# Batch 0 of a fused attention and two-layer kernel: causal mask moved into a TensorE matmul

## The chip, the cores and the metric

One core of a Trainium2 chip runs the whole program in one launch. The metric is device time in microseconds (us). The engines are called by the names of the profile: PE (TensorE matmuls), PEld (its weight loads), DVE (VectorE), ACT (ScalarE), POOL (GpSimd), SP (the queue that issues the DMAs).

## The reference

Attention over 4 batches, 8 heads, 576 positions and 64 columns a head, with a bias made of a running sum, then two feed-forward layers on the result (512 to 1536 gated to 512, then 512 to 2048 to 512). The part that the change touches:

```python
s_pos = np.maximum(s, 0.0)
cum = np.cumsum(s_pos, axis=-1)
bias = -(cum[:, :, :, None] - cum[:, :, None, :])
scores = np.where(causal, -1000000000.0, scores + np.minimum(bias, 0.0))
scores = scores - np.max(scores, axis=-1, keepdims=True)
attn = np.exp(scores)
attn = attn / (np.sum(attn, axis=-1, keepdims=True) + 1e-09)
return np.matmul(attn, v)
```

`causal` is true where the key comes after the query.

## The kernel before

The program has three stages on one timeline. First comes the attention of batch 0 alone (the opening). Then the first layer of batch b runs on PE with the attention of batch b + 1 woven in. The second layer closes. The change is in the opening and in one helper.

**Units and slots.** Two heads make a pair, a pair is cut into half A (query tiles 0, 1 and 2 of `TILES`: 64, 128 and 128 queries, keys 0 to 320) and half B (tiles 3 and 4, 128 queries each, keys 0 to 576). Batch 0 has 8 such units, A and B by turns. `body` (lines 837 to 858) walks through slots 0 to 9 with an order written out by hand for every engine (`manual_schedule`); each engine takes its instructions in that order. Slot u (`first_slot`, line 763) does three things at once: scores of unit u, transposes of unit u - 1, values of unit u - 2. An even slot therefore has A scores, B transposes and A values, an odd slot B scores, A transposes and B values.

**The way of one unit.** `masks` (line 192) lets POOL copy the running sum `c` into a tile `e` with everything after the query replaced by a huge negative number (`affine_select`, one instruction a tile and head; in batch 0 over the full width of the tile). `score_mm` (line 206) multiplies queries by keys on PE; the two heads have 64 rows each and run side by side in the two halves of the array, in fp32, so each matmul is two passes in the trace. `score_min` (line 223) adds scores and `e` on DVE and finds the row's extreme value, `expo` (line 243) takes the exponential and the row sum on ACT, `inverse` (line 259) adds up and inverts the sum on DVE, `normal` (line 283) scales the rows on POOL. `turn_mm` (line 289) transposes the result on PE (L302 over the full array, L309 into 64-column halves of it), `turned` (line 319) copies it out of PSUM on ACT and DVE, `value_mm` (line 329) multiplies by the values, and `x_high` and `x_low` split the result into two parts (ACT, then DVE).

**Weights.** Beside this, the first weight block (chunk 0) is unpacked from 64-bit numbers in four pieces (`decode`, `unpack`, line 406: first step on ACT at L409, second on ACT at L410, two on DVE at L412 and L415) after slots 2, 3, 5 and 6, and cut into a high and a low part (`w_cut`, line 491) after slots 4 and 7. `gate` (line 540; its matmuls stand in `mm3`, L522 to L524) begins the first layer when slot 9 starts.

Slot 7 (`u == H - 1`) has an order of its own at its end: the copies of slot 6's transposes (`turned`), then the DVE part of a decode, then `inverse` of tile 4, then `normal` of tile 4 on POOL.

Of the kernel before, what the change touches and what calls it, by code (L numbers as in the profile page):

```python
# [8 lines left out]
F32 = mybir.dt.float32  # L9
F32R = mybir.dt.float32r  # L10
U32 = mybir.dt.uint32
AF = mybir.ActivationFunctionType
ALU = mybir.AluOpType
# [53 lines left out]
def kernel(  # L67
# [42 lines left out]
    def copy(eng, out, in_, scale=1.0):  # L110
        if eng == "a":
            act_last[:] = [nc.scalar.activation(out=out, in_=in_, func=AF.Copy, scale=scale).ins]  # L112
        elif eng == "v":
            nc.vector.tensor_scalar(out=out, in0=in_, scalar1=scale, scalar2=None, op0=ALU.mult)
        else:
            nc.gpsimd.tensor_scalar(out=out, in0=in_, scalar1=scale, scalar2=1.0, op0=ALU.mult, op1=ALU.mult)
# [30 lines left out]


    st = {}
    first_v, first_z, sums = [], [], []  # L150

    def zeros():
        for n in range(2):
            t = zero_p.tile([P, P], F32, tag=f"v0_{n}", name="vz")
            nc.vector.memset(t, 0.0)
            first_v.append(t)
        first_z.append(zero_p.tile([P, P], F32, tag="z0", name="z0"))
        nc.vector.memset(first_z[0], 0.0)
        for n in range(6):
            sums.append(zero_p.tile([P, 2, 2], F32, tag=f"l{n}", name="ls"))  # L160
            nc.vector.memset(sums[n], 1.0e-9)
# [30 lines left out]
    def masks(b, g, half, tiles=None):  # L192
        c = st[b, g, "qkc"][1]
        es = st.setdefault((b, g, half, "e"), {})
        for i in HALF[half][0] if tiles is None else tiles:
            q0, r = TILES[i]
            g0, wd = (GATE[i] if b > 0 else 0), q0 + r
            e = e_p.tile([P, 2, S], F32, tag="e", name="e")
            for hd in range(2):
                nc.gpsimd.affine_select(  # L200
                    out=e[:r, hd, g0:wd], in_=c[:r, hd, g0:wd], pattern=[[-1, wd - g0]], compare_op=ALU.is_ge,
                    fill=-8.0 * QMASK, base=q0 - g0, channel_multiplier=1,
                )
            es[i] = e

    def score_mm(b, g, half):
        t = st[b, g, "qkc"][0]
        if b == 0:
            banks = [[ps_m.tile([P, 512], F32, tag="m", name="psc") for _ in range(2)] for _ in range(2)]
        else:  # L210
            banks = [ps_a.tile([P, 2, 512], F32, tag="a", name="psc") for _ in range(2)]
            banks = [[p[:, 0], p[:, 1]] for p in banks]
        st[b, g, half, "s"] = banks
        for i, bank, o, c0, n in PACK[half]:
            q0 = TILES[i][0]
            for hd in range(2):
                d0 = hd * D
                nc.tensor.matmul(  # L218
                    out=banks[bank][hd][:, o : o + n], lhsT=t[d0 : d0 + D, 0, q0 : q0 + P],
                    rhs=t[d0 : d0 + D, 1, c0 : c0 + n], start=True, stop=True,  # L220
                )

    def score_min(b, g, half, i):
        c, e, banks = st[b, g, "qkc"][1], st[b, g, half, "e"][i], st[b, g, half, "s"]
        r, g0 = TILES[i][1], (GATE[i] if b > 0 else 0)
        m = [None, None]
        for k, bank, o, c0, n in PACK[half]:
            if k != i:
                continue
            for hd in range(2):  # L230
                for k0, end, gate in ((c0, min(g0, c0 + n), c), (max(g0, c0), c0 + n, e)):
                    if k0 >= end:
                        continue
                    m2 = sm_p.tile([P, 1], F32, tag="m", name="m")
                    nc.vector.tensor_tensor_reduce(  # L235
                        out=e[:r, hd, k0:end], in0=banks[bank][hd][:r, o + k0 - c0 : o + end - c0],
                        in1=gate[:r, hd, k0:end], scale=-0.125,
                        scalar=3.0e38 if m[hd] is None else m[hd][:r], op0=ALU.add, op1=ALU.min, accum_out=m2[:r],
                    )
                    m[hd] = m2  # L240
        st[b, g, half, "m", i] = m
# [38 lines left out]
            else:  # L280
                copy("g", z[:r, hd * D : hd * D + D], e[:r, hd, :D], f)

    def normal(b, g, half, i):
        r, e, rl = TILES[i][1], st[b, g, half, "e"][i], st[b, g, half, "l", i]
        for hd in range(2 if i > 0 or b == 0 else 0):
            x = e[:r, hd, D if b > 0 else 0 : sum(TILES[i])]
            copy("g", x, x, rl[:r, hd : hd + 1])

    def turn_mm(b, g, half):
        tiles, base, n = HALF[half]  # L290
# [28 lines left out]
    def turned(b, g, half, k):  # L319
        n = HALF[half][2]  # L320
        ps, _, pt = st[b, g, half, "p"]
        pt[k] = pt_p.tile([P, 2, 512], F32, tag="pt", name="pt")
        w = WIDE[half][k]
        if w is None:
            copy("av"[k], pt[k][:, 0, :n], ps[k][:, 0, :n])
        else:
            copy("av"[k], pt[k][:, :, :w], ps[k][:, :, :w])
# [35 lines left out]
    def x_low(b, g, half):  # L363
        _, base, n = HALF[half]
        xp, acc = xin[b][g][:, :, base : base + n], st.pop((b, g, half, "x"))
        nc.vector.tensor_tensor(out=xp[:, 1], in0=acc[:, :n], in1=xp[:, 0].bitcast(F32), op=ALU.subtract)
# [38 lines left out]

    def unpack(zz, t, k, part="av"):
        lo, hi = t[:, :, 0], t[:, :, 1]
        if "a" in part:
            nc.scalar.activation(out=zz, in_=hi.bitcast(F32), func=AF.Copy, scale=2.0**-112)  # L409
            nc.scalar.activation(out=k, in_=lo, func=AF.Copy, scale=0.937 * 2.0**-29)  # L410
        if "v" in part:
            nc.vector.scalar_tensor_tensor(  # L412
                out=k, in0=zz.bitcast(U32), scalar=3, in1=k, op0=ALU.logical_shift_left, op1=ALU.bitwise_or
            )
            nc.vector.scalar_tensor_tensor(  # L415
                out=zz.bitcast(U32), in0=hi, scalar=0x80000000, in1=k, op0=ALU.bitwise_and, op1=ALU.bitwise_or
            )
# [345 lines left out]
    def first_slot(u):  # L763
        x = units[u] if u < H else None
        y = units[u - 1] if 1 <= u <= H else None
        z = units[u - 2] if 2 <= u <= H + 1 else None
        tiles = HALF[x[2]][0] if x else []
        after = HALF[units[u + 1][2]][0]
        if x:
            if u > 0:  # L770
                fetch(u)
            score_mm(*x)
            if u < H - 1:
                masks(*units[u + 1], after[:1])
        if z:
            value_mm(*z)
        if y:
            turn_mm(*y)
        for k, i in enumerate(tiles):
            score_min(*x, i)  # L780
            expo(*x, i)
            if z and k == (1 if x[2] == "A" else 0):
                x_high(*z)
            if z and k == len(tiles) - 1:
                x_low(*z)
            if k > 0:
                inverse(*x, tiles[k - 1])
                if u < H - 1:
                    first_keys(*x, tiles[k - 1])
                normal(*x, tiles[k - 1])  # L790
        if z and not x:
            x_high(*z)
            x_low(*z)
        if u == H - 1:
            turned(*y, 0)
            turned(*y, 1)
        if u - 1 in DECODE:
            decode(0, DECODE.index(u - 1), "v")
        if u == H - 1:
            inverse(*x, tiles[-1])  # L800
        if y and u != H - 1:
            turned(*y, 0)
            turned(*y, 1)
        if x:
            if u < H - 1:
                inverse(*x, tiles[-1])
                masks(*units[u + 1], after[1:])
                first_keys(*x, tiles[-1])
            normal(*x, tiles[-1])

    def w_ahead(c):
        wst.pop(c - 1, None)
# [7 lines left out]
    def body():  # L820
# [16 lines left out]
        for u in range(H + 2):  # L837
            if u == H + 1:
                for e in range(2):
                    decode(1, e)  # L840
                gate(0, 0, 0, *both[0])
            first_slot(u)
            if u in DECODE:
                decode(0, DECODE.index(u), "a")
            if u == H:
                masks(*units[H])
            if u in SPLIT:
                w_cut(0, SPLIT.index(u))
            if u == H - 1:
                for i in HALF["B"][0]:  # L850
                    first_keys(*units[u], i)
            if u == SPLIT[0]:
                w_piece(1, 0)
            if u == SPLIT[1]:
                for i in range(1, 4):
                    w_piece(1, i)
            if u >= H:
                w_store(0, u - H)
# [209 lines left out]
```

## Time and profile before

| | us |
|---|---|
| median of the three runs shown (1008.34, 1010.0, 1375.38) | 1010.0 |
| the profiled execution's own time | 1007.44 |
| its span, first to last instruction | 1005.7 |
| PE busy | 990.5 (98%) |
| DVE, ACT, POOL busy | 561.8, 521.8, 594.2 |

The profile is of one execution. A row of the timeline gives the start and the length of a run of like instructions on one engine; for PE the end is modelled and matmuls overlap, so work is read from the start of one row to the start of the next. A granted clock of 1.00 is 2.4 GHz, 0.50 is 1.2 GHz.

### The profile page before, as it was taken

To read this page: it belongs to the slowest core of one execution; us is meant where nothing else is said; L and a number is where in the kernel's file an instruction comes from. 1 tells how busy PE (TensorE), PEld (TensorE's weight loads), DVE (VectorE), ACT (ScalarE), POOL (GpSimd) and SP (SyncE) were. 2 spreads that over 40 slices of the span, in tenths; PEclk is the share of its full clock that TensorE was granted. 3 is DMA by queue.
4 is the path that set the end of the run, shared out by engine and by line. 5 is a ranking of instruction groups with operands and counts; after the bars stand their busy time and mean duration, and the time that the engine had idled before them with its cause. 6 is when DMAs were issued, how large, how long until landed. Compare 5 with 4: busy or idle time off the path is not lost.

```text
span 1005.7 us, 19494 instructions
## 1 busy us (share of the span) xinstructions
PE 990.5 (98%) x6924; PEld 930.9 (93%) x6924; DVE 561.8 (56%) x1408; ACT 521.8 (52%) x1266; POOL 594.2 (59%) x749
## 2 busy tenths in 40 slices
PE   8989999999999999999999999999999999999998
PEld 6578899899898899899899999999999999999998
DVE  5877667635635545545542223366666667665555
ACT  5869878525755535665542543244534335543333
POOL 6966757605866646756551665356567458674445
PEclk9999999999999999999999999999999999999999
DMA  8789789757798799776768676797767866896662
GB/s 234 203 251 340 250 302 282 256 181 266 262 302 269 257 320 309 277 245 230 260 235 315 253 293 247 276 386 290 293 230 281 318 223 247 297 342 233 244 223 106
DMA packets 81618, 267.17 MB, mean 266 GB/s; under 512 B 9904, under 2 KB 29360, under 8 KB 66160
## 3 DMA queue, kind: packets, MB, share of 16 engines
q1 hardware_dynamic: 81376, 265.73, 75.7%
q8 instruction: 54, 0.88, 0.3%
q14 instruction: 44, 0.36, 0.1%
q10 hardware_dynamic: 144, 0.20, 0.1%
HBM read 208.15 MB, written 57.75 MB: 264 GB/s over the span
## 4 chain that ended last, share of the span: by engine, by line
PE 89%; ACT 3%; DVE 2%; issue 2%; DMA 2%; POOL 2%; POOLq 0%; SPq 0%; DVEq 0%; ACTq 0%
PE pgv L522 9%; PE pgv L523 8%; PE pgv L524 8%; PE pu L668 6%; PE pu L664 6%; PE pu L667 6%; PE po L709 6%; PE po L710 6%; PE po L711 6%; PE po L522 5%; PE po L523 5%; PE po L524 5%; PE pv L351 4%; PE psc L218 4%; PE ptr L302 3%
## 5 line engine op out<-in xcount | busy, mean ns | idle before, releaser
L522 PE MATMUL pgv<-xt,wt 128*128 128x288 f32 x768 | 230.1, 300 | 1.6 <-DVE u L533 1.3
L523 PE MATMUL pgv<-xt,wt 128*128 128x288 f32 x768 | 226.6, 295 | 0.0
L524 PE MATMUL pgv<-xt,wt 128*128 128x288 f32 x768 | 226.5, 295 | 0.0
L641 POOL TENSOR_TENSOR h<-u,h 128x384 fp32r<-128x384 f32 x72 | 74.8, 1039 | 142.0 <-ACT h L112 134.1
L522 PEld LDWEIGHTS pgv<-xt,wt 128*128 128x128 f32 x768 | 144.5, 188 | 13.2 <-DVE m L235 6.3
L523 PEld LDWEIGHTS pgv<-xt,wt 128*128 128x128 f32 x768 | 144.6, 188 | 0.0
L524 PEld LDWEIGHTS pgv<-xt,wt 128*128 128x128 f32 x768 | 144.5, 188 | 0.0
L112 ACT ACTIVATE h<-u 128x288 fp32r<-128x288 f32 (+1 forms) x168 | 79.7, 474 | 94.8 <-DVE u L534 93.7
L536 POOL TENSOR_TENSOR h<-u,h 128x288 fp32r<-128x288 f32 x96 | 79.8, 834 | 82.3 <-ACT h L112 78.5
L522 PE MATMUL po<-h,wt 128*128 128x288 f32 x384 | 114.8, 299 | 0.0
L523 PE MATMUL po<-h,wt 128*128 128x288 f32 x384 | 113.1, 294 | 0.0
L524 PE MATMUL po<-h,wt 128*128 128x288 f32 x384 | 113.0, 294 | 0.0
L709 PE MATMUL po<-h,wt 128*128 128x384 f32 x336 | 112.4, 335 | 0.0
L710 PE MATMUL po<-h,wt 128*128 128x384 f32 x336 | 112.3, 334 | 0.0
L711 PE MATMUL po<-h,wt 128*128 128x384 f32 x336 | 112.3, 334 | 0.0
L668 PE MATMUL pu<-x,wt 128*128 128x384 f32 x330 | 111.7, 339 | 0.0
L664 PE MATMUL pu<-x,wt 128*128 128x384 f32 x330 | 111.7, 339 | 0.0
L667 PE MATMUL pu<-x,wt 128*128 128x384 f32 x330 | 111.7, 339 | 0.0
L641 POOL TENSOR_TENSOR h<-t,h 128x384 fp32r<-128x384 f32 x96 | 107.0, 1134 | 5.5 <-ACT h L112 5.5
L255 ACT ACTIVATE e<-e,m 64x64 f32<-64x64 f32 (+4 forms) x160 | 88.3, 554 | 30.6 <-DVE m L235 29.8
L670 ACT ACTIVATE s<-pu 128x384 f32<-128x384 f32 x48 | 23.6, 492 | 149.6 <-PE pu L668 149.6
L720 DVE TENSOR_TENSOR acc<-po,acc 128x384 f32<-128x384 f32 x144 | 76.8, 557 | 36.2 <-PE po L711 35.6
(114 smaller groups left out, 2192.0 us busy)
## 6 DMA issues: line engine op xcount, KB each, us to landing
wt<-w_d SPq DMA_DIRECT2D x54, 1024.0 KB, 7.0
wt<-wu_d SPq DMA_DIRECT2D x48, 1024.0 KB, 9.1
wt<-wu_d SPq DMA_DIRECT2D x47, 768.0 KB, 6.5
r<-in_w_dram SPq DMA_DIRECT2D x36, 512.0 KB, 6.4
w_d<-wt SPq DMA_DIRECT2D x18, 1024.0 KB, 8.3
r<-in_w_dram SPq DMA_DIRECT2D x64, 256.0 KB, 7.2
qkr<-in_qk_dram SPq DMA_DIRECT2D x32, 288.0 KB, 8.3
cumb<-cum_d SPq DMA_DIRECT2D x15, 576.0 KB, 9.4
```

Source lines behind the costliest of these rows:

```text
L255: nc.scalar.activation(out=e[:r, hd, :wd], in_=e[:r, hd, :wd], func=AF.Exp, bias=m[hd][:r], scale=-1.0, accum_out=put[hd],)
L522: nc.tensor.matmul(out=ps[:, :n], lhsT=a, rhs=xh, start=(k == 0), stop=False)
L523: nc.tensor.matmul(out=ps[:, :n], lhsT=a, rhs=xl, start=False, stop=False)
L524: nc.tensor.matmul(out=ps[:, :n], lhsT=c, rhs=xh, start=False, stop=(k == last))
L536: engines[LO[ph]].tensor_tensor(out=lo, in0=u, in1=hi.bitcast(F32), op=ALU.subtract)
L641: nc.gpsimd.tensor_tensor(out=h[:, 1], in0=u, in1=h[:, 0].bitcast(F32), op=ALU.subtract)
L664: nc.tensor.matmul(out=o, lhsT=a, rhs=x[:, 0, kk], start=fresh and kk == 0, stop=False, skip_group_check=True)
L667: nc.tensor.matmul(out=o, lhsT=a, rhs=x[:, 1, kk], stop=False, **more)
L668: nc.tensor.matmul(out=o, lhsT=c, rhs=x[:, 0, kk], stop=kk == 1, **more)
L709: nc.tensor.matmul(out=ps, lhsT=a, rhs=h[:, 0], start=fresh, stop=False, skip_group_check=True)
L710: nc.tensor.matmul(out=ps, lhsT=a, rhs=h[:, 1], stop=False, **more)
L711: nc.tensor.matmul(out=ps, lhsT=c, rhs=h[:, 0], stop=e == 1, **more)
```

## The change

In batch 0 POOL no longer makes masked copies of the running sum. Two constant tiles are made at the start: an identity and a triangle (0 up to the query, -8 x 2^30 after it), both rounded to fp32r. After the scores of each block that holds the diagonal, PE adds identity x triangle to the 64 or 128 columns on the diagonal, for each head, over the full 128 rows of the array. DVE then reads the running sum `c` itself. The first step of the four chunk 0 decodes goes from ACT to POOL. At the end of the opening, the inverse of the last tile of slot 7 stands ahead of the transposes' copies, its second head is scaled on ACT, and the second `w_cut` of chunk 0 goes from behind slot 7 into slot 8.

```diff
+        tri = z_p.tile([P, P], F32, tag="z", name="tri")
+        nc.gpsimd.affine_select(
+            out=tri, in_=first_z[0], pattern=[[-1, P]], compare_op=ALU.is_ge, fill=-8.0 * 2.0**30, base=0,
+            channel_multiplier=1,
+        )
+        for src in (ident, tri):
+            diag.append(z_p.tile([P, P], F32R, tag="z", name="diag"))
+            nc.vector.tensor_scalar(out=diag[-1], in0=src, scalar1=1.0, scalar2=None, op0=ALU.mult)
...
-            g0, wd = (GATE[i] if b > 0 else 0), q0 + r
+            g0, wd = GATE[i], q0 + r
             e = e_p.tile([P, 2, S], F32, tag="e", name="e")
-            for hd in range(2):
+            for hd in range(2 if b > 0 else 0):
                 nc.gpsimd.affine_select(
...
+            lo, end = max(q0, c0), min(q0 + TILES[i][1], c0 + n)
+            for hd in range(2 if b == 0 and lo < end else 0):
+                nc.tensor.matmul(
+                    out=banks[bank][hd][:, o + lo - c0 : o + end - c0], lhsT=diag[0], rhs=diag[1][:, lo - q0 : end - q0],
+                    start=False, stop=True, skip_group_check=True,
+                )
...
-        r, g0 = TILES[i][1], (GATE[i] if b > 0 else 0)
+        r, g0 = TILES[i][1], GATE[i] if b > 0 else S
...
-    def normal(b, g, half, i):
+    def normal(b, g, half, i, eng="gg"):
...
-            copy("g", x, x, rl[:r, hd : hd + 1])
+            copy(eng[hd], x, x, rl[:r, hd : hd + 1])
...
+        if part == "a":
+            copy("g", zz, hi.bitcast(F32), 2.0**-112)
+        elif "a" in part:
+            nc.scalar.activation(out=zz, in_=hi.bitcast(F32), func=AF.Copy, scale=2.0**-112)
         if "a" in part:
-            nc.scalar.activation(out=zz, in_=hi.bitcast(F32), func=AF.Copy, scale=2.0**-112)
             nc.scalar.activation(out=k, in_=lo, func=AF.Copy, scale=0.937 * 2.0**-29)
...
+        if u == H:
+            w_cut(0, 1)
         if u == H - 1:
+            inverse(*x, tiles[-1])
             turned(*y, 0)
             turned(*y, 1)
         if u - 1 in DECODE:
             decode(0, DECODE.index(u - 1), "v")
-        if u == H - 1:
-            inverse(*x, tiles[-1])
...
-            normal(*x, tiles[-1])
+            normal(*x, tiles[-1], "gg" if u < H - 1 else "ga")
...
-            if u in SPLIT:
-                w_cut(0, SPLIT.index(u))
+            if u == SPLIT[0]:
+                w_cut(0, 0)
```

On PE, from the scores of slot 0 to the first transposes (`psc` are scores in PSUM, `qkr` queries and keys, `ptr` transposes), before the change:

```order
L218 MATMUL psc<-qkr 128x64 x2
L218 MATMUL psc<-qkr 128x192 x2
L218 MATMUL psc<-qkr 128x320 x2
L218 MATMUL psc<-qkr 128x448 x2
L218 MATMUL psc<-qkr 128x64 x2
L218 MATMUL psc<-qkr 128x512 x2
L302 MATMUL ptr<-ident,e 128x128 x6
```

and after it (`diag` are the two constant tiles):

```order
L226 MATMUL psc<-qkr 128x64 x2
L232 MATMUL psc<-diag 128x64 x2
L226 MATMUL psc<-qkr 128x192 x2
L232 MATMUL psc<-diag 128x128 x2
L226 MATMUL psc<-qkr 128x320 x2
L232 MATMUL psc<-diag 128x128 x2
L226 MATMUL psc<-qkr 128x448 x2
L232 MATMUL psc<-diag 128x128 x2
L226 MATMUL psc<-qkr 128x64 x2
L232 MATMUL psc<-diag 128x64 x2
L226 MATMUL psc<-qkr 128x512 x2
L232 MATMUL psc<-diag 128x64 x2
```

Each pair of score matmuls is followed by a pair of mask matmuls: six in two slots, so 24 pairs or 48 matmuls in the opening.

On POOL, in slots 3 to 5 (`e<-e,rl` scales rows, `e<-cumb` makes a mask, `wt<-wraw,wt` is the low part of `w_cut`), before the change:

```order
L116 TENSOR_SCALAR e<-e,rl 128x576 x2
L200 AFFINE_SELECT e<-cumb 128x448 x2
L116 TENSOR_SCALAR e<-e,rl 64x64 x2
L116 TENSOR_SCALAR e<-e,rl 128x192 x2
L200 AFFINE_SELECT e<-cumb 128x576 x2
L116 TENSOR_SCALAR e<-e,rl 128x320 x2
L501 TENSOR_TENSOR wt<-wraw,wt 128x1024
L200 AFFINE_SELECT e<-cumb 64x64 x2
L116 TENSOR_SCALAR e<-e,rl 128x448 x2
L200 AFFINE_SELECT e<-cumb 128x192 x2
L200 AFFINE_SELECT e<-cumb 128x320 x2
L116 TENSOR_SCALAR e<-e,rl 128x576 x2
```

and after it (`wraw<-r` is the decode's first step):

```order
L116 TENSOR_SCALAR e<-e,rl 128x576 x2
L116 TENSOR_SCALAR wraw<-r_201 128x512
L116 TENSOR_SCALAR e<-e,rl 64x64 x2
L116 TENSOR_SCALAR e<-e,rl 128x192 x2
L116 TENSOR_SCALAR e<-e,rl 128x320 x2
L518 TENSOR_TENSOR wt<-wraw,wt 128x1024
L116 TENSOR_SCALAR e<-e,rl 128x448 x2
L116 TENSOR_SCALAR e<-e,rl 128x576 x2
```

The mask instructions are gone from between the scalings.

On DVE, at the end of slot 7 (`l` and `rl` are row sums and their inverses, `pt` a transposes' copy, `dk` and `wraw` a decode), before the change:

```order
L366 TENSOR_TENSOR xt<-pv,xt 128x256
L265 TENSOR_REDUCE l<-ls 128x2
L268 RECIPROCAL rl<-l 128x2
L114 TENSOR_SCALAR pt<-ptr 128x320
L412 SCALAR_TENSOR_TENSOR dk<-wraw,dk 128x512
L415 SCALAR_TENSOR_TENSOR wraw<-r_197,dk 128x512
L265 TENSOR_REDUCE l<-ls 128x2
L268 RECIPROCAL rl<-l 128x2
```

and after it:

```order
L380 TENSOR_TENSOR xt<-pv,xt 128x256
L279 TENSOR_REDUCE l<-ls 128x2
L282 RECIPROCAL rl<-l 128x2
L279 TENSOR_REDUCE l<-ls 128x2
L282 RECIPROCAL rl<-l 128x2
L114 TENSOR_SCALAR pt<-ptr 128x320
L429 SCALAR_TENSOR_TENSOR dk<-wraw,dk 128x512
L432 SCALAR_TENSOR_TENSOR wraw<-r_205,dk 128x512
```

The second sum and inverse, those of the last tile, now stand ahead of the copy and the decode.

## Rows read from the trace of the kernel before

**Rows 1.** Stretches: length, then busy time (instructions) of PE, PEld, DVE, ACT, POOL; clock, DMA

```profile
100.00:1005.70 905.70, 900.91 (x6248) 862.22 (x6246) 486.86 (x1150) 448.27 (x1079) 523.59 (x620) 1.00 0.75 267
```

**Rows 2.** Waits between 8.5 and 62 us: us in total, times, longest

```profile
PE ptr L302 <- POOL e L116: 5.1, 8, 1.4
POOL e L116 <- DVE rl L268: 4.6, 3, 2.4
```

**Rows 3.** Timeline of PE in the opening: start, length, instruction, count, wait before

```profile
8.54 1.36 PE L218 MATMUL psc<-qkr 64*128 64x64 f32 x12
...
14.85 0.33 PE L302 MATMUL ptr<-ident,e 128*128 128x128 f32 x1 [1.43 <-POOL e L116]
...
17.10 2.51 PE L218 MATMUL psc<-qkr 64*128 64x64 f32 x12
...
20.89 2.01 PE L302 MATMUL ptr<-ident,e 128*128 128x128 f32 x14
...
23.41 2.10 PE L218 MATMUL psc<-qkr 64*128 64x448 f32 x12
...
35.78 2.10 PE L218 MATMUL psc<-qkr 64*128 64x448 f32 x12
37.81 1.73 PE L351 MATMUL pv<-pt,vrb 128*64 128x256 f32 x16
...
39.91 0.88 PE L302 MATMUL ptr<-ident,e 128*128 128x128 f32 x6
...
41.80 1.36 PE L218 MATMUL psc<-qkr 64*128 64x64 f32 x12
43.09 0.76 PE L351 MATMUL pv<-pt,vz 128*64 128x320 f32 x4
...
44.43 0.44 PE L302 MATMUL ptr<-ident,e 128*128 128x128 f32 x2
...
48.11 2.10 PE L218 MATMUL psc<-qkr 64*128 64x448 f32 x12
...
55.48 0.76 PE L351 MATMUL pv<-pt,vz 128*64 128x320 f32 x4 [0.60 <-DVE pt L114]
...
61.82 0.61 PE L522 MATMUL pgv<-xt,wt 128*128 128x288 f32 x1
```

**Rows 4.** Stretches of the opening and behind it, columns as in rows 1

```profile
16.20:19.60 3.40, 3.40 (x22) 2.20 (x23) 1.27 (x8) 1.94 (x6) 3.25 (x9) 0.50 1.05 338
...
60.60:63.90 3.30, 3.30 (x18) 2.81 (x17) 1.88 (x2) 2.83 (x5) 3.30 (x12) 0.50 1.02 427
```

**Rows 5.** POOL by form between 8 and 61 us: busy us, mean ns

```profile
L200 POOL TENSOR_SCALAR_AFFINE_SELECT e<-cumb 128x576 f32<-128x576 f32 x8 | 5.1, 662 | 0.2 <-PE ptr L309 0.2
L200 POOL TENSOR_SCALAR_AFFINE_SELECT e<-cumb 128x448 f32<-128x448 f32 x8 | 4.7, 610 | 0.0
```

**Rows 6.** PE around the scores of batch 1 between two fp32r runs

```profile
74.58 0.29 PE L524 MATMUL pgv<-xt,wt 128*128 128x288 f32 x1
74.80 1.36 PE L218 MATMUL psc<-qkr 64*128 64x64 f32 x12
76.08 0.40 PE L522 MATMUL pgv<-xt,wt 128*128 128x288 f32 x1
76.32 0.29 PE L523 MATMUL pgv<-xt,wt 128*128 128x288 f32 x1
76.45 0.29 PE L524 MATMUL pgv<-xt,wt 128*128 128x288 f32 x1
```

**Rows 7.** The forms of decode and scaling up to 130 us

```profile
L409 ACT ACTIVATE wraw<-r 128x512 f32<-128x512 f32 x22 | 14.3, 668 | 2.4 <-POOL wt L501 1.3 <-DMA r<-in_w_dram 0.8 <-issue 0.3
...
L116 POOL TENSOR_SCALAR e<-e,rl 128x512 f32<-128x512 f32 x4 | 2.7, 707 | 0.0
```

**Rows 8.** POOL at the end of the opening

```profile
57.29 1.99 POOL L116 TENSOR_SCALAR e<-e,rl 128x576 f32<-128x576 f32 x2 [1.70 <-DVE rl L268]
```

**Rows 9.** Waits of PE between 62 us and the end

```profile
PE pgv L522 <- DVE u L533: 1.3, 1, 1.3
```

More of the change, by code (lines that the diff above doesn't have):

```diff
@@ L149 @@
     st = {}
-    first_v, first_z, sums = [], [], []
+    first_v, first_z, sums, diag = [], [], [], []
     def zeros():
```

## Prediction

> **What bounds the kernel now.** I read the stretches first. From 100 us to the end PE is busy for 900.91 of 905.70 us at clock 1.00 [rows 1], so nothing that the change does to POOL, ACT or DVE there can show; only the opening, up to the first matmul of the first layer at 61.82 us, has anything to give. The waits of that opening come next: PE waits for POOL's scaling 5.1 us in all, and POOL in its turn 4.6 us for DVE's inverse [rows 2]. Then the timeline of PE, read from start to start [rows 3]. A pair of slots lasts 12.37 us (23.41 to 35.78). Taken where PE hardly waits, an even slot is A scores 1.29 (41.80 to 43.09), A values 1.34 (to 44.43) and B transposes 2.52 (20.89 to 23.41), together 5.15; an odd slot is B scores 2.03 (35.78 to 37.81), B values 2.10 (to 39.91) and A transposes 1.89 (to 41.80), together 6.02. So 11.17 of the 12.37 us are PE's own work, and only 1.2 us a pair is a wait that POOL could give back. That is the point to see: POOL ends the waits, but PE stands right behind it. The rest of what is lost lies at the two ends: 1.43 us before the transposes at 14.85 [rows 3], and twice a stretch at clock 0.50, that is 1.2 GHz, from 16.2 to 19.6 and from 60.6 to 63.9 us, each after PE had stood waiting for transposes' inputs [rows 4].
>
> **The masks taken from POOL.** In batch 0 each tile has two selects, 40 in all, in five widths of eight each. The two widest forms alone cost 5.1 and 4.7 us [rows 5], 2.4 us a pair of slots. PE gets its 1.2 us a pair from this and no more. In the first slots it counts for more: the last scaling of slot 0 stood behind two selects of 0.66 us [rows 5], so the transposes that wait at 14.85 [rows 3] and their followers can go up to 1.3 us sooner; I take 0.7, since the scores in front of them end later.
>
> **The masks put on PE.** 48 matmuls are added in 24 pairs, three pairs a slot. No fp32r matmul of 128 columns is in the trace, and none that cuts into the scores, so I build its price from the places where PE goes from full-height fp32r matmuls to the two half-height rows of scores and back [rows 6]. A stream of 288 columns takes 0.13 us from start to start (76.32 to 76.45). Before the scores it takes 0.22 (74.58 to 74.80): 0.09 us to empty the array. After the scores the first takes 0.24 (76.08 to 76.32): 0.11 more, because its weights are not loaded ahead. So a mask pair costs 0.09 to enter, 0.11 for its first weights, 0.11 for the second weights (a second load of that length behind the first), and 0.06 for 128 columns at the rate of 0.13 for 288: 0.37 us. The way back to scores costs 0.09 and about 0.10 for the scores' weights. The third pair of a slot has no way back, since the values that follow change the form of the array anyway. A slot: 3 x 0.37 + 2 x 0.19 = 1.49, less 0.03 for each pair of 64 columns and about 0.1 where the scores' weights were waited for already: 1.36. Eight slots: 10.9 us more on PE. It is on the path, as an odd or even slot of PE then lasts 7.38 and 6.51, a pair 13.9 us, above the 12.37 of now. Other engines have more room than before, so no wait is added on top.
>
> The bounds of this price. Below: both mask matmuls cost a weight load each and nothing for the change of form, 0.22 a pair and 5.3 us in all. Above: a narrow fp32r matmul runs at the rate of fp32, whose 128-column passes take 0.11 each and need two; a pair is then 0.6 us with its entry, 0.2 to 0.27 more, and the whole 5.6 us more, 16.5 us. I take 10.9, since the fp32r rows [rows 6] are the nearest of kind and their price of change is measured.
>
> On the change of form itself the Trainium skill (TensorEngine Tiling (Array Packing), Key Properties) says that switching the tiling mode drains TensorE. By the drain alone, without exposed weights, 24 pairs would cost some 5 us less and this would be the faster rival below; the trace has both parts, 0.09 and 0.11 us.
>
> The constants cost nothing: one select on POOL and two small copies on DVE at the start, which nothing waits for until the first scores at 8.54 [rows 3].
>
> **Decode on POOL.** ACT loses four instructions of 668 ns [rows 7], some 0.6 us each in a row of others. POOL gets four of the same size: 128x512 takes 707 ns there [rows 7], perhaps twice that with every second word read. Against 9.8 us taken off in two forms alone, 3 to 6 us on POOL is hidden behind PE's own work. If PE were not the bound, ACT's 2.4 us could count as a gain, or POOL's 6 as a loss of what exceeds the masks taken away. No DMA changes its place in the opening's queue; the loads of the raw pieces now wait for POOL as well, which is done before DVE's part.
>
> **The last slots.** Now slot 7's inverse stands behind a copy and a decode, so POOL scales the last tile from 57.29 to 59.28, after 1.70 us of waiting [rows 8]. That is 9.1 us after the last scores (48.11 + 2.03) [rows 3]. Without the 1.70 of waiting and with one head on ACT (1.0 less) it is 6.4 us at most. The new scores end at 54.2 (below), so the rows are there by 60.6 at the latest, and PE comes to them at 60.1, with the other tile's transposes first: at most a few tenths late, taken as nothing. The 0.60 us for the copy before the values at 55.48 [rows 3] stays. The second `w_cut` is queued in slot 8 on ACT ahead of the copy of the last transposes. It lies beside 2.52 us of transposes on PE, and its result is wanted by the 13th matmul of the first layer, 12 x 0.13 = 1.6 us later, so I cost it at nothing; if that cover is gone, the cost is what it is late.
>
> **The sum.** Starts of the slots' scores, before and then after: slot 0 8.54 and 8.54; slot 1 11.2 after; slot 2 17.10 and 16.5 (A transposes from 14.6, at full clock); slot 3 23.41 and 23.0; then 7.38 and 6.51 in turn to slot 7 at 50.8 (48.11 before). There 3.39 for scores (2.03 + 1.36), 2.10, 1.89, the wait of 0.60, 1.34 and 2.52: the first layer begins at 62.6 against 61.82, 0.8 us later. PE has then worked without a long wait, so I expect clock 1.00 where it was 0.50 from 60.6 to 63.9 [rows 4]: half of 3.3 us back, 1.65. Net -0.9 us. Against the profiled 1007.44 that is 1006.5. The two ordinary runs shown are 0.9 and 2.6 above the profiled one (1008.34, 1010.0, the latter the median); I add the smaller, 0.9: **1007.4 us**, no change that a measurement would tell (2% of this kernel, some 20 us, is about what one can).
>
> **The rivals.**
> 1. Slower: the mask matmuls run at fp32's rate (0.27 us more for a pair of 128 columns). For it: their columns are fewer than those of any fp32r matmul in the trace. Against: the same type streams 288 columns in 0.13. It makes the first layer start at 68.2, net +4.7, with the 0.9 some 1013. It decides from 0.04 us more a mask pair than I took.
> 2. Faster: the change of form is nearly free, because the weights of the mask are the same in all 48 and its drain hides. For it: POOL's waits do go. Against: rows 6. Net -6.5, some 1001.8.
> 3. The time regained is lost behind the opening: at about 97 us PE waits 1.3 us for DVE [rows 9], and the weights of the first layer come by a DMA queue that is full from 60.6 to 63.9 (1.02) [rows 4]. Or PE still stands long enough that the clock falls as before. Either leaves 0 to +0.8, 1008.3 to 1009.1.
>
> **Chances.** Forecast 0.45, rival 1 0.2, rival 2 0.2, rival 3 0.15. All four lie within 2%: nothing here reaches 20 us either way, since the opening's PE work before masks is some 43 of its 53.3 us (four of each kind above, three B values). Only something unseen leaves the band: 0.015 faster, 0.97 within, 0.015 slower. The range takes rivals 1 and 2 in: 1000.5 to 1013.5; the forecast's own is 1004 to 1010.
>
> **What would show it.** Right: a pair of slots near 13.9 us with no wait of PE for POOL, 0.09 and 0.11 us around each mask pair, the first layer at 62 to 63, clock 1.00 after it. Wrong: a pair of slots under 12.4 us (rival 2), or mask matmuls 0.2 us apart (rival 1), or the 0.50 clock still there (rival 3).

## The result and the profile after

The changed kernel is slower by 0.9%, clear of the noise but inside 2%: 1017.47 us median of 12 runs (1012.24 to 1025.7) against 1009.01 for the kernel before, a ratio of 1.0089 [1.007, 1.0107]. The forecast was 1007.4 with a range from 1000.5 to 1013.5. The profiled execution took 1017.69 us, its span 1015.9 us against 1005.7. The traces lie further apart (10.2 us) than the medians (8.5), because the profiled execution of the kernel before, 1007.44 us, is faster than all 12 of its other runs.

First the part that came out as forecast. PE's timeline over one pair of slots, where the clock was full (start and length; read from start to start):

```profile
27.73 1.02 PE L226 MATMUL psc<-qkr 64*128 64x448 f32 x4
28.68 0.44 PE L232 MATMUL psc<-diag 128*128 128x128 f32 x2
29.05 0.44 PE L226 MATMUL psc<-qkr 64*128 64x64 f32 x4
...
33.26 0.88 PE L316 MATMUL ptr<-ident,e 128*128 128x128 f32 x6
34.30 0.92 PE L323 MATMUL ptr<-ident,e 64*64 64x64 f32 x12 [0.16 <-DVE l L279]
...
41.73 1.02 PE L226 MATMUL psc<-qkr 64*128 64x448 f32 x4
```

From one odd slot's scores to the next it is 14.00 us (27.73 to 41.73; forecast 13.9, [rows 3] give 12.37). A mask pair of 128 columns takes 0.37 (28.68 to 29.05), as was built from [rows 6]. And the 5.1 us that PE waited for POOL [rows 2] are gone: no such wait of PE is among those of the opening (8.5 to 65 us). There the others now wait, DVE for PE and POOL behind DVE:

```profile
engine line waited for: us in total, times, longest us
POOL e L116 <- DVE rl L282: 14.1, 9, 4.7
...
DVE e L249 <- PE psc L232: 10.2, 9, 4.4
```

Then the part that did not. The stretches of PE in the changed kernel, cut at slot 0, the first transposes, slots 3, 5 and 7, the first matmul of the first layer and the 217th (columns: stretch, length, busy, granted clock, DMA share, GB/s):

```profile
core 0: us, PE busy (x), PEclk, DMA share, GB/s
8.91:18.81 9.90, 9.90 (x37) 0.56 0.92 293
18.81:27.73 8.92, 8.88 (x71) 0.91 1.06 225
27.73:41.73 14.00, 13.80 (x115) 1.00 0.56 160
41.73:55.72 13.99, 13.79 (x114) 1.00 0.45 141
55.72:68.02 12.30, 11.14 (x96) 1.00 0.71 214
68.02:113.10 45.08, 39.57 (x287) 0.96 0.84 289
```

There are two losses. The scores and masks of slots 0 and 1 ran at 0.56 of full speed with PE busy all the time (9.90 of 9.90 us). And from the first layer's start to its 217th matmul it took 45.08 us with 5.5 us of idle time. In the kernel before the same matmuls took 11.29 + 28.89 = 40.18 us; its stretches (PE's busy time stands first, the clock third from the end):

```profile
61.82:73.11 11.29, 11.29 (x86) 10.52 (x85) 10.51 (x14) 7.64 (x14) 6.49 (x11) 0.91 0.72 243
73.11:102.00 28.89, 27.36 (x203) 24.37 (x202) 22.35 (x78) 25.38 (x71) 19.90 (x28) 1.00 0.93 325
```

So the first layer began 6.2 us late (68.02 against 61.82) and lost 4.9 us more by the 217th matmul. Those 11.1 us hold the whole loss; behind that matmul the two kernels run nearly alike, the changed one 0.9 us shorter, and the spans end 10.2 us apart.

### The profile page after: what moved, and what is told of

It is laid out like the page before. It is cut to its first block, busy times and chain, and to the rows that moved or that the text cites. A ratio compares the mean times of both kernels' runs of the same rounds, so it can differ in the third digit from the quotient of the medians.

```text
span 1015.9 us, 19484 instructions
## 1 busy us (share of the span) xinstructions
PE 1003.3 (99%) x6972; PEld 939.3 (92%) x6972; DVE 560.9 (55%) x1410; ACT 521.6 (51%) x1263; POOL 583.2 (57%) x713
## 4 chain that ended last, share of the span: by engine, by line
PE 92%; DMA 2%; ACT 2%; POOL 1%; DVE 1%; issue 1%; SPq 0%; DVEq 0%; POOLq 0%; ACTq 0%
PE pgv L539 9%; PE pgv L541 9%; PE pgv L540 9%; PE pu L681 6%; PE pu L685 6%; PE pu L684 6%; PE po L726 6%; PE po L728 6%; PE po L727 6%; PE po L539 5%; PE pv L365 5%; PE psc L226 5%; PE po L540 5%; PE po L541 5%; PE ptr L316 3%; DMA r<-in_w_dram 1%
## 5 line engine op out<-in xcount | busy, mean ns | idle before, releaser
L116 POOL TENSOR_SCALAR e<-e,rl 128x128 f32<-128x128 f32 (+8 forms) x135 | 72.9, 553 | 65.0 <-DVE rl L282 47.5
```

## The experiments

The theory at this point had two parts: full-height mask pairs cost what was forecast but let the clock fall at the start, and something in the reordered end costs PE time behind the opening. The rivals: the decode on POOL is to blame, or weights and not the change of form are the price.

**One part at a time.** `masks_only` keeps the masks on PE and takes back the other two parts; `rest_only` is its opposite. The core of `masks_only`:

```diff
-        if part == "a":
-            copy("g", zz, hi.bitcast(F32), 2.0**-112)
...
-        if u == H:
-            w_cut(0, 1)
```

and of `rest_only`:

```diff
-            for hd in range(2 if b > 0 else 0):
+            for hd in range(2):
                 nc.gpsimd.affine_select(
```

> Only the masks go to PE; the decode's first step is on ACT again and the last slots have their old order. Theory (the masks' price on PE, and a lower clock at the start): a pair of slots lasts 14.0 us as in the full change, the clock falls to 0.50 soon after the first mask matmuls, and the time is 1012 to 1020. Rival (the price comes from the decode on POOL and the new order at the end): the time is at most 2 us above the kernel before.

> The masks go back to POOL; the decode's first step stays on POOL, and the last slots keep the new order. Theory (masks are the price): a pair of slots lasts 12.4 to 13.5 us, PE waits for POOL more than the 5.1 us of before, the clock stays 1.00 up to 16 us as before, and the time is 1006 to 1012. Rival (the other two parts cause the loss behind the opening): PE still has a gap of over 3 us for the weights near 100 us, and the time is 1012 or more.

Masks alone: 1018.51 us, 1.0087 [1.0059, 1.0115]; pair of slots 13.99; 0.50 from 10.14 to 20.38 us. The rest alone: 1011.88, 1.0026 [1.0013, 1.0038], although its first layer began 1.2 us earlier than before's (60.64). The theory of `masks_only` held in all its points. Of `rest_only`'s, the pair of slots, the clock up to 16 us and the time came as its theory said, but PE waited less for POOL than before (3.9 us), and the gap near 100 us is its rival's. So the masks carry the low clock, but they are not all of it: with the rest alone PE had the same gap of 3.87 us before the 193rd matmul of the first layer as the full change, with masks alone only 1.79. (A gap is read here from the start of the last piece of work ahead of it, so 0.43 us of it are work.) The gap in `rest_only`:

```profile
96.17:100.04 3.87, 0.43 (x4) 0.85 0.56 233
```

Both parts lose, in two places.

**No mask matmuls, and fewer changes of form.** A change of form is the step from half-height matmuls to full-height ones or back. `none` leaves the mask matmuls out. `grouped` issues a slot's scores first and its masks behind them. In that order part of batch 0's scores is changed, so both kernels serve for their times alone. The second loop of `grouped`:

```diff
+        for i, bank, o, c0, n in PACK[half]:
+            q0 = TILES[i][0]
             lo, end = max(q0, c0), min(q0 + TILES[i][1], c0 + n)
             for hd in range(2 if b == 0 and lo < end else 0):
```

> The full change without the 48 mask matmuls: batch 0 is computed without its causal mask; the constants are still made. Theory (0.37 + 0.19 us a mask pair, and the clock at the start falls because the mask pairs break up the scores): a pair of slots lasts 11.2 us, the clock stays at 1.00 up to 16 us, the first layer starts near 50 us and the time is 995 to 1002. Rival (something else than the mask matmuls lowers the clock at the start): 0.50 still from about 10 us on, and the time is above 1003.

> The full change, but each slot issues its three score blocks first and its three mask pairs behind them, so PE changes form once a slot and not three times. Theory (0.19 for each way back and 0.09 for each entry): 16 entries and ways back go, some 0.28 us each, 4.5 us in all; a pair of slots lasts 12.9 us, and the time is 3 to 6 us under the full change. Rival 1 (weights are the price, not the change of form): a pair stays at 13.7 or more. Rival 2 (DVE gets its first scores later and becomes the bound): PE waits for DVE's or POOL's rows, over 2 us in the opening.

The stretch of a pair of slots on PE, all at full clock, in `none`:

```profile
34.03:45.28 11.25, 10.97 (x102) 1.00 0.86 208
```

and in `grouped`:

```profile
35.72:48.67 12.95, 12.57 (x115) 1.00 0.51 155
```

With 13.79 for the full change, six mask pairs cost 13.79 - 10.97 = 2.82 us, 0.47 each and 11.3 in the opening (forecast 10.9); four of those six entries less save 1.22, 0.3 each, as expected. The clock did not fall in slots 0 and 1 of either profile. But `none`, with 11 us of work less on PE than the full change, took 1007.22 us, 0.9992 [0.9976, 1.0009], and so missed the 995 to 1002 of its theory: it began its first layer at 56.19, 5.6 us before the old kernel and not at 50, and was only 1.6 us ahead at the 217th matmul. Here the loss behind the opening shows by itself: 4.0 us, without any mask on PE. `grouped` (1012.43, 1.003 [1.0018, 1.0041]) had the same gap of 3.87 us.

**Which part loses behind the opening.** `end_only` gives the decode back to ACT, `decode_only` gives the last slots their old order back.

> The full change, but with the decode's first step on ACT again: masks on PE and the new order of the last slots stay. In the trace of the full change PE waits 3.4 us for the weights' unpacking at 104 us, in that of masks alone 1.3 us, and the first layer's start is 2.8 us earlier with the full change. Theory A (the new last slots cause both): the first layer starts 2 to 3 us earlier than with masks alone, and PE has the gap of 3.9 us before the 193rd matmul of the first layer; time 1012 to 1020, as the full change. Theory B (the decode on POOL causes the loss behind): the gap is 1.8 us, and by the 217th matmul this kernel is 2 to 4 us ahead of the full change at like clock.

> The full change, but with the old order of the last slots: masks on PE and the decode's first step on POOL stay. Theory A (the new last slots cause the loss behind the opening): the first layer starts at 70 to 71 us (where the clock is low from 10 to 20 us), the gap before its 193rd matmul is 1.8 us, and the time is that of masks alone. Theory B (the decode on POOL does it): that gap is 3.9 us, and the time is 2 to 4 us above masks alone at like clock.

Theory A held in the traces. `end_only` (1020.32, 1.0107 [1.0078, 1.0136]) began its first layer at 68.04 and had a gap of 3.89 us; `decode_only` (1013.07, 1.0059 [1.003, 1.0087]) began at 70.82 and had 1.79. At the 217th matmul they stood at 113.05 and 110.78 us, within 0.05 of the full change (113.10) and of masks alone (110.78). Up to there the decode on POOL costs and brings nothing. The times did not come as theory A had them (1020.32 for at most 1020, and 1013.07 where masks alone took 1018.51): with full-height masks the clock differs from run to run, as the runs under **Where the clock falls** show, so the medians of these few runs do not rank the kernels.

**The order behind the opening.** Behind slot 9 only PE's order is written by hand; a planner orders the other engines. `cutback` is the full change with one piece of the end put back, the second cut behind slot 7.

```diff
-        if u == H:
-            w_cut(0, 1)
...
-            if u == SPLIT[0]:
-                w_cut(0, 0)
+            if u in SPLIT:
+                w_cut(0, SPLIT.index(u))
```

> The full change, but the second cut of chunk 0 goes back behind slot 7 as in the kernel before; masks, decode on POOL and the rest of the new end stay. With it POOL's order behind the opening is the old one again: a product's low part ahead of the four selects for the third unit of batch 1, and not behind them. Theory (that order is what costs PE 3.9 us before the 193rd matmul of the first layer): the gap is 1.8 us, the first layer's start is within 1 us of the full change at like clock, and from there to the 217th matmul it takes 3 to 4 us less. Rival (the gap comes from an early start of the first layer itself, whatever the order): the gap stays at 3 us or more.

The gap went from 3.86 to 1.77 us, as expected, and from the first layer's start to the 217th matmul it took 40.83 us, 4.25 less than the full change. POOL's timeline ahead of the gap, in the full change:

```profile
99.98 1.16 POOL L116 TENSOR_SCALAR e<-e,rl 128x384 f32<-128x384 f32 x2
101.09 1.36 POOL L208 TENSOR_SCALAR_AFFINE_SELECT e<-cumb 128x320 f32<-128x320 f32 x4
102.41 0.81 POOL L553 TENSOR_TENSOR h<-u,h 128x288 fp32r<-128x288 f32 x1
```

and in `cutback`, where the low part of a product of the first layer, `h`, goes ahead of the selects:

```profile
94.69 1.15 POOL L116 TENSOR_SCALAR e<-e,rl 128x384 f32<-128x384 f32 x2
95.80 0.81 POOL L553 TENSOR_TENSOR h<-u,h 128x288 fp32r<-128x288 f32 x1
96.56 1.36 POOL L208 TENSOR_SCALAR_AFFINE_SELECT e<-cumb 128x320 f32<-128x320 f32 x4
```

Read the waits down the chain. DVE's timeline in the full change: its next step waits for that `h`, and the weights' unpacking comes behind it.

```profile
103.25 0.45 DVE L550 SCALAR_TENSOR_TENSOR u<-th,pgv 128x288 f32<-128x288 f32 x1 [3.42 <-POOL h L553]
...
107.56 0.68 DVE L432 SCALAR_TENSOR_TENSOR wraw<-r,dk 128x512 uint32<-128x512 uint32 x1
```

PE's timeline there, with the wait for that unpacking:

```profile
103.50 1.36 PE L226 MATMUL psc<-qkr 64*128 64x64 f32 x12
108.29 0.40 PE L539 MATMUL pgv<-xt,wt 128*128 128x288 f32 x1 [3.43 <-DVE wraw L432]
```

In `cutback` DVE waited 2.01 us for `h`, and PE 1.34 us, there for the step at L550 and not for the unpacking:

```profile
101.68 0.40 PE L539 MATMUL pgv<-xt,wt 128*128 128x288 f32 x1 [1.34 <-DVE u L550]
```

From DVE's step to PE's next matmul it is the same in both: 108.29 - 103.25 = 5.04 and 101.68 - 96.65 = 5.03. So the 2.1 us by which the gap is longer arise ahead of DVE's step, and 1.3 of them are the four selects that POOL now does first (101.09 to 102.41). The order on DVE and ACT differs there too; what each of the engines' orders is worth was not tried apart.

The gap has a sequel. PE's stretches in the gap and behind it, in the full change:

```profile
104.43:108.29 3.86, 0.43 (x4) 1.00 0.20 82
109.12:112.53 3.41, 3.41 (x16) 0.50 0.59 168
```

and in `cutback`:

```profile
99.91:101.68 1.77, 0.43 (x4) 1.00 0.82 332
101.68:105.09 3.41, 3.41 (x26) 1.00 0.80 244
```

Behind the long gap the clock is 0.50, and 16 matmuls go in the time in which 26 go in `cutback`. All six profiled kernels with a gap of 3.9 us show a stretch at 0.50 that begins in the gap or within 1 us of its end (the full change, `rest_only`, `none`, `grouped`, `end_only`, `same_form`), and none with a gap of 1.8.

`cutback`'s time was 1014.7 us, 1.007 [1.0045, 1.0095], with eight runs between 1010.28 and 1021.29 and mean clocks between 0.989 and 1.00. Its profiled run had the full clock throughout, and its stretches up to slot 5 show what the change costs without the fall at the start:

```profile
7.91:14.05 6.14, 6.14 (x37) 1.00 0.89 256
14.05:22.28 8.23, 8.19 (x72) 1.00 1.01 278
22.28:36.27 13.99, 13.79 (x115) 1.00 0.95 213
```

The same 37 matmuls that took 9.90 us at 0.56 take 6.14 here. Up to slot 3 it is 14.37 us against 18.82: 4.45 us are the clock's.

**The masks in the scores' own form.** Each mask product is cut in two over the 64 rows of its own head; a second pair of constants has the halves swapped. `same_form` is the full change with this, `sf_cutback` also puts the cut back, `sf_invback` leaves the cut in slot 8 and puts the inverse back (`diag[2]`, `diag[3]` are the swapped identity and triangle).

```diff
-            for hd in range(2 if b == 0 and lo < end else 0):
+            for k in range(2 if b == 0 and lo < end else 0):
+                k0 = max(lo, q0 + D) if k and lo == q0 else lo
+                if k0 >= end:
+                    continue
+                for hd in range(2):
+                    d0, x = hd * D, 2 * (hd ^ k)
+                    nc.tensor.matmul(
+                        out=banks[bank][hd][:, o + k0 - c0 : o + end - c0], lhsT=diag[x][d0 : d0 + D],
+                        rhs=diag[x + 1][d0 : d0 + D, k0 - q0 : end - q0], start=False, stop=True, skip_group_check=True,
+                    )
```

> The full change, but each mask product is cut in two over the 64 rows of its own head (the constants get a second pair with their halves swapped), so that the two heads' masks run side by side in the same half-height form as the scores and PE never changes form for them. Theory (0.09 to enter, 0.09 and 0.10 for the way back are the change of form): the pair costs some 0.3 us instead of 0.37 + 0.19, a pair of slots lasts 12.3 to 12.8 us, the first layer starts at 60 to 63 us, and the time is 4 to 7 us under the full change at like clock. Rival (weights are the price: there are up to four half-height weights a block now): a pair of slots stays at 13.7 or more.

> Masks in the scores' own form (two half-height products for each head, with swapped constants), and the second cut of chunk 0 behind slot 7 as in the kernel before; the decode on POOL and the rest of the new end stay. Theory (the price on PE was the change of form, the loss behind was the order): the first layer starts at 57 to 59 us, the gap before its 193rd matmul is 1.8 us, the lead over before at the 217th matmul is 2 to 4 us, and the time is 1004 to 1007. Rival (an earlier first layer waits for its weights, whatever the order): no more than 1 us of the lead is left by the 217th matmul, and the time is that of before.

> Masks in the scores' own form and the second cut of chunk 0 in slot 8, but the inverse of slot 7's last tile behind the transposes' copies and the decode again, and both its heads scaled on POOL. POOL's order behind the opening is the old one here too. Theory (the inverse is what brought the first layer forward, the order is what lost it): the first layer starts 1 to 3 us later than with the cut put back, the gap before its 193rd matmul is 1.8 us, and the time is 1006 to 1009. Rival (the cut in slot 8 by itself makes the weights late): the gap is over 3 us.

PE's timeline in `same_form`, the first blocks of an odd slot:

```profile
33.98 1.02 PE L232 MATMUL psc<-qkr 64*128 64x448 f32 x4
34.49 0.66 PE L243 MATMUL psc<-diag 64*128 64x128 f32 x4
34.98 0.42 PE L232 MATMUL psc<-qkr 64*128 64x64 f32 x4
```

and its stretch of a pair of slots:

```profile
33.98:46.11 12.13, 11.93 (x122) 1.00 0.56 168
```

Six blocks cost 11.93 - 10.97 = 0.96 us, 0.16 each where the full-height pair costs 0.47, although there are more weights to load. The change of form was most of the price. The Trainium skill (TensorEngine Tiling (Array Packing), Key Properties) says that switching the tiling mode drains TensorE; these rows agree that a switch costs, 0.3 us a block for the drains on both sides and the weights that then lie bare, but no run tells the two apart.

`same_form` took 1008.68 us, 1.0003 [0.9993, 1.0014]: it began the first layer at 57.49, earlier than expected, and had lost its lead of 4.3 us by the 217th matmul, as `none` lost most of its own. With the old order there the lead stays: `sf_cutback` 1005.47, 0.9974 [0.9963, 0.9985], and `sf_invback` 1005.46, 0.997 [0.9958, 0.9982], are both faster than the kernel before, by 0.3%. Their first layers began at 59.61 and 58.21, and the gap was 1.75 in both. So it is not an early start of the first layer that makes the gap long, nor the cut in slot 8 alone, which `sf_invback` has too: the long gap came only with both, the cut in slot 8 and the inverse ahead with its second head on ACT. Against the expectation the old inverse did not make `sf_invback` later than `sf_cutback`, and its time lies below the 1006 to 1009 that were given; the old cut costs `sf_cutback` a wait of 1.6 us for `xt` in the last transposes. Stretches of `sf_invback`, slot 3 to 5, slot 7 to the first layer, and up to its 217th matmul:

```profile
21.23:33.60 12.37, 11.96 (x122) 1.00 1.01 221
...
45.73:58.21 12.48, 10.45 (x100) 1.00 0.90 279
58.21:98.25 40.04, 37.76 (x287) 1.00 0.90 311
```

**Where the clock falls.** `first_sf` is `cutback` with the masks of units 0 and 1 in the scores' form and those of units 2 to 7 at full height.

> As the kernel with the cut put back (full-height mask pairs, clock between 0.989 and 1.00 over its runs), but the first pair of heads, units 0 and 1, takes its masks in the scores' own form; the other six units keep the full-height pairs. Theory (what spreads the runs is a clock that falls during the first two slots, where full-height mask pairs cut into the first scores): the mean clock of every run is 0.995 or more, the profiled clock has no 0.50 between 10 and 20 us, and the time is 1008 to 1012 with a spread of under 4 us. Rival (full-height mask pairs lower the clock wherever they stand in the opening): some runs still have a mean clock of 0.990 or less, and times of 1017 and more.

It took 1010.43 us, 1.0018 [1.0006, 1.003]. All 12 runs had a mean clock of 0.997 or more; their spread of 4.6 us is a little more than the 4 expected. So it is in the first two slots that full-height mask pairs cost the clock, as far as these runs tell (`cutback`, five of whose eight runs were at 0.995 or less, ran on another chip; there the two kernels with all masks in the scores' form had 0.997 or more in all 20 runs). PE's stretches in its profiled run, up to the first transposes, to slot 3 and to slot 5:

```profile
8.12:12.96 4.84, 4.60 (x46) 1.00 0.86 260
12.96:21.94 8.98, 8.62 (x72) 1.00 1.00 289
21.94:35.94 14.00, 13.79 (x115) 1.00 0.98 225
```

The mean clocks of all runs say the same. Five kernels have full-height pairs that cut into the first scores: the full change (0.988 to 0.998, one run 0.939), `masks_only` (0.989 to 0.998), `end_only` (0.988 to 0.996), `decode_only` (0.990 to 0.998), `cutback` (0.989 to 1.00). All others lie at 0.992 or above in every run, 80 runs in seven kernels. The times follow the clock: the full change's two runs at 0.998 took 1012.24 and 1012.66 us, the four at 0.988 1021.58 to 1024.14. The profiled run, at 0.993, stands between.

## Why the prediction was wrong

**Right: the price on PE.** 0.37 for a mask pair and 0.19 for the way back were forecast as 10.9 us in all; the busy time says 11.3. A pair of slots lasts 14.0 (13.9), and PE no longer waits for POOL. Rival 1 (matmuls at fp32's rate) and rival 2 (the change of form nearly free) are out: the mask matmuls follow each other in 0.16 us, and the same masks without a change of form cost 0.31 us a block less. The decode's first step takes POOL 666 ns, not up to twice 707. That the first layer began at 68.02, beside the 68.2 of rival 1, is chance: the price that rival 1 rests on did not come.

**Wrong, first step: "A transposes from 14.6, at full clock".** They began at 18.81 and slot 2 at 21.16 instead of 16.5. PE had no wait there; in the profiled run it ran at 1.2 GHz from 10.1 to 20.4 us. The prediction tied a low clock to PE standing idle, since both stretches of [rows 4] followed a wait, and concluded that fewer waits mean more clock. Here the clock fell while PE was never idle. Taken at full clock the schedule of the prediction is good: `cutback` has slot 2 at 15.71 and slot 3 at 22.28 (forecast 16.5 and 23.0, from first scores 0.6 us later). The step is worth 4.45 us in the profiled run; with 0.4 us of a later start (8.91 for 8.54), 0.2 over the next two pairs and 0.5 behind slot 7, less 0.1, that is the distance from 62.6 to 68.02. The later start is not the constants': over the profiled kernels the first scores start between 7.81 and 9.19 us, with constants or without (8.54 before, 8.91 in `rest_only`).

**Wrong, second step: the second `w_cut` "I cost it at nothing".** Its cover was judged by the 13th matmul of the first layer, which indeed did not wait. But the new end, this cut together with the earlier inverse, let a planner order POOL, DVE and ACT differently 30 to 40 us later. From the first layer's start to the 217th matmul the change lost 4.9 us where it was to gain 1.65: 2.1 in the longer gap, some 1.6 by the 0.50 that follows it (4.81 us from the 193rd to the 217th matmul for 3.26 before), 1.9 in two shorter gaps (1.2 us at 78 us that was not there before, 1.24 at 87 us for 0.52; all six kernels with the whole new end have both, the others neither) and 0.3 spread, less 1.0 that the full clock at the first layer's start did give (12 matmuls in 1.68 us for 2.65). The expected 1.65 was oversized too: of the 3.4 us at 0.50 [rows 4] only those behind 61.82 lie in the first layer. Rival 3 named this place, with at most 0.8 us; it counted only what had been regained as what could be lost.

**Why no range held it.** Up to the first layer's start the forecast is missed by 5.4 us, 4.45 of them the first step's, and behind it by 6.5; with the forecast's -0.9 this gives the 11.1 of the trace at that point, to a tenth. The range was drawn from the price of the masks alone, which was the one term that was well known. Three of the twelve runs, with mean clocks of 0.997 and 0.998, took 1012.24 to 1012.79 us and lie inside it: where the clock holds at the start, the second step alone does not leave the range.

## What to carry to other kernels

When work moves onto the engine that bounds a stage, look at the form in which it arrives: the same masks cost 11.3 us as full-height products between half-height ones and 3.8 in the neighbours' own form. An order written by hand that ends earlier hands a different picture to the planner of what follows, so compare the other engines' orders behind the edit before you put an edit there at nothing. And where a clock can fall, carry a run at either level in the range: one trace at full clock does not show that it stays.

## What was not expected of the hardware

A fully busy PE can be given the lower clock: 0.50 from 10.13 to 20.37 us in the full change, with 10.00 of 10.00 us busy between 10.25 and 20.25, and no idle time from 6.72 to 10.13, before it fell. The full change:

```profile
10.25:20.25 10.00, 10.00 (x32) 0.50 0.95 284
```

It happened with mask pairs at full height in the first two slots, and, by the mean clocks, not in all runs. In the four profiled ones where it did the first scores began at 8.87 to 8.91 us; `cutback`, with the same masks, began at 7.91 and kept 1.00, and `rest_only`, with no mask on PE, began at 8.91 and had 1.00 beyond 16.95:

```profile
8.91:10.13 1.22, 1.22 (x13) 1.00 0.95 340
10.13:13.54 3.41, 2.94 (x16) 1.00 0.91 253
13.54:16.95 3.41, 1.80 (x18) 1.00 1.00 329
```

From 10.13 on PE was less busy there than in the full change, and kept its clock. So the mask pairs matter. That the moment of the start matters too is only suggested, by one profile of `cutback`; no run varied it alone. On the moment, the Trainium skill (TensorE: Matmul & The Clock Gate, Part 1) says that the clock's changes are not tied to the kernel's start, so that runs of one kernel differ; the spread of the full change's runs, mean clocks of 0.988 to 0.998, agrees. Why the clock fell with the pairs, and not with the scores alone, stays open.
